# Attention stage of an mLSTM, MoE and MLP kernel: weight groups one per chunk from the second to the tenth, the inter bank read ahead of the state sums, q and k laid out contiguously

## The chip, the cores and the metric

The kernel runs on one core of one Trainium2 chip. The metric is device time in microseconds (us) of one execution; lower is better. One execution was also recorded by the hardware profiler, and all rows below come from that record. Engines are named as in the profile: PE (TensorE matmul; PEld is its weight load), DVE (VectorE), ACT (ScalarE), POOL (GpSimd), SP (SyncE, which here only issues DMAs).

## What is computed

Three layers in a row, all with f32 inputs. The change touches only the first, an mLSTM attention over B=2 batches, H=8 heads, S=768 steps, head size D=40:

```
for t in range(S):
    m_new = max(f[t] + m, i[t])
    C = exp(f[t] + m - m_new) * C + exp(i[t] - m_new) * outer(v[t], k[t])
    n = exp(f[t] + m - m_new) * n + exp(i[t] - m_new) * k[t]
    y[t] = sigmoid(o[t]) * (C @ q[t]) / max(abs(n . q[t]), 1)
```

Its output, 1536 tokens of 320 values, goes through a noisy top-2 mixture of 8 experts (`out += w * relu(x @ w1[e]) @ w2[e]`, hidden size 1024), and that result through a 2048-wide MLP with a relu6 gate.

## The kernel before

The order of the work on every engine is the order in which the program is written: nothing reorders it, and an engine that waits holds up all that stands behind it in its own queue. The recurrence is computed in chunks of 64 steps, 12 chunks, both batches side by side on the 128 partitions (64 rows each). Chunk n of the main loop (n = 0 to 9; the last two chunks are written out after it) does this:

- `pmul(n+1)` (L261): DVE multiplies the scores of chunk n+1 by their decay matrix, which frees the scores' PSUM bank for chunk n+2.
- `step(2)`: two pieces of the routing generator `route`, which handles two chunks' tokens at a time. It is started at the end of chunks 2, 4, 6, 8, so its first pieces stand in the odd chunks: a copy of the logits (L430), Abs and Exp on ACT (L433, L434), and DVE's `w<-u` (L439), which needs them.
- `inter(n)` (L281): 32 matmuls of q and k against the state `Sb`, written to bank 3, the inter bank. The same bank is used in each chunk, so PE may write it only after `norm_eg` of the chunk before has read it.
- `state(n)` (L291, L297): 32 matmuls of k and v into two banks, and two DVE sums that update `Sb`; then `decay` on POOL (L270).
- `load(n+3)` (L136): q, k, kv and the output gates of three chunks ahead, on SP's queue.
- `norm2(n-1)` (L361, L362, L364): tokens x of the chunk before, and their store to DRAM.
- `scores(n+2)` (L231), `values(n)` (L308), `expo(n+2)` (L238, L240, exponent on ACT L243), `xpose(n-1)` (PE transposes L388, ACT copies L390, L391) and `logits(n-1)` (L402).
- `scatter` (L414, L415): routing indices on POOL.
- weights of expert 0: `w_hi` casts one group on ACT (L593 or L598) into a high part, `w_lo` subtracts on DVE (L594 or L599) to get the low part, `w_load` loads the next group from DRAM (L589) into one of four `raw` buffers. A load into a buffer waits until the low part made from it is done. All three stand in chunks 3 to 7, `w_load` alone also before the loop and in chunks 0 to 2.
- `kscale(n+2)` (L255): eight ACT multiplies, in chunks 3 to 8.
- `norm_eg(n)` (L327): DVE reads the inter bank; `norm_pv(n)` (L334 to L346): DVE adds the values bank and prepares the denominator.
- `gate(n+1)`: a DVE max (L353), then Exp, Ln, Exp on ACT (L354 to L356).

On DVE, `norm_eg(n)` stands behind `w_lo`; `w_lo` needs ACT's cast, and this stands on ACT behind the copies of `xpose`, which need PE's transposes:

```
        scatter(3 if n == 8 else 2)
        if 3 <= n < 8:
            w_hi()
            w_lo()
        if n < 8:
            w_load()
        ...
        kscale(n + 2)
        norm_eg(n)
        step(2)
        norm_pv(n)
        gate(n + 1)
```

The mixture of experts starts after the loop and a tail that normalises, routes and gathers the last tokens; its first matmuls (L845) need expert 0's five weight groups.

Of the kernel before, what the change touches and what calls it, by code (L numbers as in the profile page):

```python
# [24 lines left out]
NT = 12  # L25
# [38 lines left out]
def mlstm_moe_mlp(ctx, tc, qk, kv, on, gf, gf6, wg, nz, w1, w2, w_in, w_out, cf, cb, cs, ci, out):  # L64
# [28 lines left out]
    identb, maskb, eyeb = cbt[:, 0:128], cbt[:, 128:192], cbt[:, 192:256]  # L93
    ltri, ones = cbt[:, 256:384], cbt[:, 384:512]

    QK = [att.tile([128, 4, 3, 128], F32, name=f"qk{i}") for i in range(4)]
    RWG = att.tile([128, 6, 2, 128], BF, name="RWG")
    Sb = att.tile([128, B, 4, V1], F32, name="Sb")
    SEL = const.tile([128, 8, B, 64], BF, name="SEL")
# [12 lines left out]

    def qk_parts(n):
        t = QK[n % 4]
        return [(t[64 * x:64 * x + 40, :, x:x + 2, :], qk[n, x]) for x in range(2)]

    def kv_part(n):
        kvt[n] = att.tile([128, H * (D + V1)], F32, name="kv", bufs=4)
# [94 lines left out]
    def step(k=1):  # L213
        for _ in range(k):
            for g_ in list(gens):
                if next(g_, "end") == "end":
                    gens.remove(g_)
# [6 lines left out]
    def scores(n, ps_=range(4)):  # L224
        q = QK[n % 4]
        if n not in s4t:
            s4t[n] = bank(3 if n == 1 else 0).rearrange("p (h t) -> p h t", h=8)
        s4 = s4t[n]
        for p in ps_:
            for b in range(B):  # L230
                T.matmul(s4[rows[b], 2 * p:2 * p + 2, :], q[:, p, 1, rows[b]], q[:, p, 0:3:2, rows[b]],  # L231
                         start=True, stop=True)

    def expo(n):
        e = bank(1)
        e3 = e.rearrange("p (h t) -> p h t", h=8)
        for b in range(B):
            T.matmul(e[rows[b]], rwg(0, n), SEL[:, :, b, :], start=True, stop=False, skip_group_check=True)  # L238
        for h in range(8):
            T.matmul(e3[:, h, :], SEL[:, h].rearrange("p b t -> p (b t)"), rwg(1, n), start=False, stop=True,  # L240
                     skip_group_check=True)
        d = att.tile([128, 8, 64], F32, name="dd", bufs=3)
        A.activation(d, e3, AF.Exp)  # L243
        Pt[n] = None, d
        if n + 1 < NT:
            k = att.tile([128, 8, D], F32, name="kt", bufs=3)
            kt[n] = k
            if n < 5:
                G.tensor_tensor(k, kvt[n][:, 0:DM].rearrange("p (h d) -> p h d", h=8),
                                d[:, :, 63:64].to_broadcast([128, 8, D]), OP.mult)  # L250
# [22 lines left out]
    def inter(n, bp=2, bi=3):  # L273
        q = QK[n % 4]
        vv = kvt[n][:, DM:].rearrange("p (h d) -> p h d", h=8)
        pv = bank(bp)[:, 0:8 * V1].rearrange("p (h d) -> p h d", h=8)
        it = bank(bi)[:, 0:8 * V1].rearrange("p (a c) -> p a c", a=4)
        for p in range(4 if n else 0):
            for x in range(2):
                for b in range(B):  # L280
                    T.matmul(it[rows[b], p, x * V1:(x + 1) * V1], q[:, p, 2 * x, rows[b]], Sb[:, b, p, :],  # L281
                             start=True, stop=True)
        y_ps[n] = (pv, it, vv)

    def state(n):
        Sd = Sds.pop(n, None)
        vv = y_ps[n][2]
        for b in range(B):
            for h in range(8):
                p, x = divmod(h, 2)  # L290
                T.matmul(stp[b][64 * x:64 * x + 40, p, :], kt[n][rows[b], h, :],  # L291
                         vv[rows[b], h, :], start=True, stop=True)
        spot[0] += 2
        step()
        for b in range(B):
            if n:
                V.tensor_tensor(Sb[:, b], Sd[:, b], stp[b], OP.add)  # L297
            else:
                V.tensor_copy(Sb[:, b], stp[b])
            step()  # L300
        if n + 2 < NT:
            decay(n + 1)
# [28 lines left out]
    def norm_pv(n):  # L331
# [15 lines left out]
        step()  # L347
        yt[n] = o, rd

    def gate(n):  # L350

        t = ont[n]
        V.tensor_scalar(t, t, -80.0, None, OP.max)  # L353
        A.activation(t, t, AF.Exp, scale=-1.0)  # L354
        A.activation(t, t, AF.Ln, bias=1.0)
        A.activation(t, t, AF.Exp, scale=-1.0)  # L356
# [49 lines left out]
    def cut_idx(e):  # L406
        assert len(scat) >= 2 * CUT[e], len(scat)
        nc.sync.dma_start(idx[(0, 3)[e]][:, 0:2, :], tab4[:, 0:2, :])
# [298 lines left out]
    def w_load():  # L707
        if pos[0] < len(queue):
            loaded.append(raw_load(queue[pos[0]][0]))
            pos[0] += 1  # L710
# [3 lines left out]
    def w_hi(k=1):  # L714
        for _ in range(k):
            los.append(queue[pos[1]][1](loaded[pos[1]]))
            pos[1] += 1

    def w_lo(k=1):
        for _ in range(k):  # L720
            los.pop(0)()
# [295 lines left out]
    load(2)  # L1017
    warm(WARM)
    scores(0)
    w_load()  # L1020
    warm(W[0])
    expo(0)
    pmul(0)
# [2 lines left out]
    decays()  # L1026
    warm(W[2])
    expo(1)
    gate(0)
    G.tensor_copy(adj, iota8)  # L1030
    warm(W[3])
    for n in range(NT - 2):
        pmul(n + 1)
        step(2)
        inter(n)
        state(n)
        if n + 3 < NT:
            load(n + 3)
        if n >= 1:
            norm2(n - 1)  # L1040
            step()
        scores(n + 2, range(2))
        values(n, range(4))
        expo(n + 2)
        values(n, range(4, 8))
        if n >= 1:
            xpose(n - 1)
        scores(n + 2, range(2, 4))
        scatter(3 if n == 8 else 2)
        if 3 <= n < 8:  # L1050
            w_hi()
            w_lo()
        if n < 8:
            w_load()
        if n + 3 >= NT:
            dummy(DUM[0], 1)
        if n >= 1:
            logits(n - 1)
        kscale(n + 2)
        norm_eg(n)  # L1060
        step(2)
        norm_pv(n)
        gate(n + 1)
        if n >= 2 and n % 2 == 0:
            gens.append(route(n // 2 - 1))
        if n == CUT[0] + 2:
            scatter(4)
            cut_idx(0)
    gate(NT - 1)
    n = NT - 2  # L1070
    pmul(n + 1)
# [162 lines left out]
def _arrays(inp):  # L1234
    import ml_dtypes
    q, k, v, o = [_np.asarray(inp[n]) for n in ('q', 'k', 'v', 'o_gate')]

    def bits(a):
        return _np.ascontiguousarray(a).view(_np.int64)

    def tr(a):
        return a.reshape(B, H // 2, 2, NT, 64, D).transpose(3, 2, 5, 1, 0, 4).reshape(NT, 2, D, H // 2, 128)

    def nat(a):
        return a.reshape(B, H, NT, 64, D).transpose(2, 0, 3, 1, 4).reshape(NT, 128, H, D)

    qt, kt = tr(q), tr(k)
    qk = _np.stack([_np.stack([qt[:, 0], kt[:, 0]], axis=3), _np.stack([kt[:, 1], qt[:, 1]], axis=3)], axis=1)
    vn = _np.concatenate([nat(v), _np.ones((NT, 128, H, 1), _np.float32)], axis=3)
    kv = _np.concatenate([nat(k).reshape(NT, 128, -1), vn.reshape(NT, 128, -1)], axis=2)  # L1250
    on = nat(o).reshape(NT, 128, H * D)
    gf = _np.stack([_np.asarray(inp[n]).reshape(16, S) for n in ('i_gate', 'f_gate')], axis=1)
    gf6 = gf.reshape(16, 2, 6, 128).transpose(0, 2, 1, 3).reshape(96, 2, 128)
    wgn = _np.zeros((384, 16), _np.float32)
    wgn[:320, :8] = inp['moe_w_gate']
    wgn[:320, 8:] = inp['moe_w_noise']
    wg = wgn.reshape(3, 128, 16).transpose(1, 0, 2)
    nz = _np.asarray(inp['moe_noise']).reshape(2, NT, 64, 8).transpose(0, 2, 1, 3).reshape(128, NT, 8)
    p = _np.arange(128)
    cf = _np.zeros((128, 147), _np.float32)  # L1260
    cf[:, 146] = -7.0 * 2 ** 30
    cf[:, :128] = _np.eye(128)
    cf[:, 128:136] = _np.arange(8)
    cf[64:, 144] = -1.0
    cf[:, 145] = 3.0
    mask = _np.where(_np.arange(64)[:, None] > _np.arange(64)[None], -1e30, 0.0)
    free = _np.concatenate([_np.arange(16, 32), _np.arange(48, 64), _np.arange(96, 128)])
    mk = _np.zeros((128, 128))
    mk[free] = _np.concatenate([mask, _np.eye(64)], axis=1)
    ltri = 8.0 * (p[:, None] < p[None])  # L1270
    cb = _np.concatenate([_np.eye(128), mk, ltri, _np.full((128, 128), 8.0)], axis=1).astype(ml_dtypes.bfloat16)
    sel = _np.zeros((128, 8, 2))
    for r in range(48):
        sel[r // 16 * 32 + r % 16, r % 8, r % 16 // 8] = 1.0
    cs = sel.reshape(128, 16).astype(ml_dtypes.bfloat16)
    ci = (_np.arange(NT)[None] * 128 + p[:, None]).astype(_np.int32)
    a = dict(qk=qk, kv=kv, on=on, gf=gf, gf6=gf6, wg=wg, nz=nz, w1=inp['moe_w1'], w2=inp['moe_w2'],
             w_in=bits(inp['moe2_w_in']).reshape(DM, 2, F).transpose(1, 0, 2).reshape(2 * DM, F), w_out=bits(inp['moe2_w_out']).reshape(2, 8, 128, DM).transpose(0, 2, 1, 3).reshape(256, 8 * DM), cf=cf, cb=cb, cs=cs, ci=ci)
    return {n: _np.ascontiguousarray(x) for n, x in a.items()}
# [16 lines left out]
```

## Time and profile before

| | us |
|---|---|
| median of 3 runs | 553.83 |
| lowest, highest of them | 552.12, 556.47 |
| the profiled execution, its own time | 558.33 |
| its span, first to last instruction | 556.5 |
| busy over the span: PE, PEld | 516.3, 460.8 |
| busy over the span: DVE, ACT, POOL | 340.5, 238.4, 127.2 |

The attention stage with its start takes about the first 120 us of the span, the tail to the first expert matmul another 16 us; the rest is the experts and the MLP. The share of busy time is a mean over stages with different limits. The granted clock is the share of TensorE's full 2.4 GHz that the chip gave: 1.00 or 0.50, and in a stretch with both something between.

### The profile page before, as it was taken

What the parts mean: (1) busy time and instruction counts of PE and PEld (TensorE: products, weight loads), DVE (VectorE), ACT (ScalarE), POOL (GpSimd) and SP (SyncE); (2) the same over time, 40 slices, a digit from 0 to 9 for tenths busy, and PEclk for the clock granted to TensorE, in tenths of its full rate; (3) what the DMA queues carried; (4) which work ended last, traced back from release to release, by engine and by line L of the source; (5) the groups of instructions that cost most, each with busy time, mean ns of one, the idle gap of its engine ahead of it and who ended that gap; (6) DMA issues with size and microseconds to landing.
All of it is one profiled execution on the core that took longest, in us unless ns stands there. A gap on an engine that the chain in (4) does not pass through costs nothing. (4 is left out here: it accounts for less than half of the span.)

```text
span 556.5 us, 11218 instructions
## 1 busy us (share of the span) xinstructions
PE 516.3 (93%) x4329; PEld 460.8 (83%) x4329; DVE 340.5 (61%) x853; ACT 238.4 (43%) x498; POOL 127.2 (23%) x165
## 2 busy tenths in 40 slices
PE   5878886996978999999999999999999999999996
PEld 2657665764978999999999989989988899999885
DVE  5354546655864487878787878547878534343433
ACT  0333555433444354545454545345654333333332
POOL 5231232525632220202020101078600100000000
PEclk9895755568988999999999999999999999999999
DMA  5793656501628667889897866976931600001011
GB/s 154 227 248 94 188 110 117 122 25 58 153 61 273 219 215 257 304 244 313 268 314 248 282 213 208 301 213 201 343 119 48 230 8 0 2 15 34 7 42 49
DMA packets 48073, 90.81 MB, mean 163 GB/s; under 512 B 7584, under 2 KB 32512, under 8 KB 48016
## 3 DMA queue, kind: packets, MB, share of 16 engines
q1 hardware_dynamic: 39976, 68.14, 40.3%
q0 software_dynamic: 6464, 19.94, 11.9%
q10 hardware_dynamic: 1576, 1.97, 1.2%
q8 instruction: 35, 0.57, 0.5%
q14 instruction: 22, 0.18, 0.1%
HBM read 66.77 MB, written 23.07 MB: 161 GB/s over the span
## 5 line engine op out<-in xcount | busy, mean ns | idle before, releaser
L860 DVE SCALAR_TENSOR_TENSOR r<-r,bank 128x512 f32<-128x512 f32 (+1 forms) x56 | 34.2, 611 | 81.7 <-ACT r L859 77.7
L845 PE MATMUL bank<-XH,SB 128*128 128x448 f32 (+3 forms) x280 | 78.9, 352 | 0.3 <-PEq L945 0.3
L848 ACT ACTIVATE hb<-bank 128x448 fp32r<-128x448 f32 (+2 forms) x80 | 37.4, 468 | 95.6 <-PE bank L845 77.9
L859 ACT ACTIVATE r<-bank,cft 128x512 f32<-128x512 f32 (+1 forms) x56 | 35.0, 626 | 96.9 <-PE bank L845 86.9
L845 PE MATMUL bank<-XL,SB 128*128 128x448 f32 (+3 forms) x192 | 68.8, 359 | 0.0
L881 PE MATMUL bank<-SB,hb 128*128 128x320 f32 x192 | 62.5, 326 | 3.0 <-ACT yo L916 1.4
L772 POOL DMA_INDIRECT XG<-Xd,idx x32 | 30.9, 966 | 133.6 <-PE bank L782 106.0
L881 PE MATMUL bank<-SA,hb 128*128 128x320 f32 x192 | 60.8, 316 | 0.0
L883 PE MATMUL bank<-SB,hb 128*128 128x320 f32 x192 | 60.1, 313 | 0.0
L882 PE MATMUL bank<-SB,hb 128*128 128x320 f32 x192 | 59.7, 311 | 0.0
L883 PE MATMUL bank<-SA,hb 128*128 128x320 f32 x192 | 59.4, 309 | 0.1
L882 PE MATMUL bank<-SA,hb 128*128 128x320 f32 x192 | 59.3, 309 | 0.0
L845 PE MATMUL bank<-XH,SA 128*128 128x448 f32 (+2 forms) x200 | 54.0, 342 | 2.0 <-ACT XH L783 2.0
L845 PEld LDWEIGHTS bank<-XH,SB 128*128 128x128 f32 x280 | 51.6, 193 | 5.1 <-issue 0.6
L845 PE MATMUL bank<-XL,SA 128*128 128x448 f32 (+2 forms) x120 | 40.9, 341 | 0.0
L845 PEld LDWEIGHTS bank<-XH,SA 128*128 128x128 f32 x200 | 37.2, 199 | 4.3 <-ACT XH L783 2.5
L881 PEld LDWEIGHTS bank<-SB,hb 128*128 128x128 f32 x192 | 36.6, 191 | 5.0 <-ACT hb L832 1.8
L594 DVE TENSOR_TENSOR SA<-raw,SA 128x1024 fp32r<-128x1024 f32 (+1 forms) x20 | 27.1, 1356 | 20.6 <-ACT SA L593 20.2
L845 PEld LDWEIGHTS bank<-XL,SB 128*128 128x128 f32 x192 | 37.0, 193 | 2.8
L882 PEld LDWEIGHTS bank<-SB,hb 128*128 128x128 f32 x192 | 36.6, 191 | 0.8
L881 PEld LDWEIGHTS bank<-SA,hb 128*128 128x128 f32 x192 | 36.1, 188 | 1.3
L882 PEld LDWEIGHTS bank<-SA,hb 128*128 128x128 f32 x192 | 36.1, 188 | 1.1
(201 smaller groups left out, 1141.3 us busy)
## 6 DMA issues: line engine op xcount, KB each, us to landing
raw<-in_w_dram SPq DMA_DIRECT2D x18, 640.0 KB
raw<-in_w_dram SPq DMA_DIRECT2D x18, 512.0 KB
craw<-in_w_in_dram SPq DMA_DIRECT2D x8, 640.0 KB
craw<-in_w_out_dram SPq DMA_DIRECT2D x8, 640.0 KB
raw<-in_w_dram SPq DMA_DIRECT2D x18, 256.0 KB
Yd<-yo SPq DMA_DIRECT2D x24, 160.0 KB
Yd<-zy SPq DMA_DIRECT2D x4, 880.0 KB
kv<-in_kv_dram SPq DMA_DIRECT2D x10, 324.0 KB
```

Source lines behind the costliest of these rows:

```text
L594: return lambda: eng.tensor_tensor(lo, t[:, 0:w], hi, OP.subtract)
L772: G.indirect_dma_start(out=XG[0:n, (u.xo + i) % 4, :], out_offset=None, in_=Xd[0:CUT[u.i] * 128] if early else Xd[:, :], in_offset=bass.In ...
L845: T.matmul(p, a, b, start=(i == 0), stop=(i == 7))
L848: A.activation(hb[:, 0:N], p, AF.Relu)
L859: A.activation(r, p, AF.Relu, bias=three)
L860: V.scalar_tensor_tensor(r, r, 6.0, p, OP.min, OP.mult)
L881: T.matmul(p, h, wh, start=s, stop=False)
L882: T.matmul(p, h, wl, start=False, stop=False)
L883: T.matmul(p, hb[:, lo:lo + 128], wh, start=False, stop=t)
```

## The change

- q and k: the SBUF tile changes from (pair, part, 128) to (part, pair, 128), and the arrays in DRAM with it, so that one partition's row of a load is one run of 1,024 values (4 KB) where it was four of 256 (1 KB). Bytes and matmuls stay.
- The weight loads move: none before the loop and none in chunk 0; one in each of the chunks 1 to 9 (before: one before the loop and one in each of the chunks 0 to 7). In a chunk they now stand ahead of `scores`.
- `w_hi` moves from chunks 3 to 7 to chunks 4 to 8, behind `kscale` and `gate`; `w_lo` of the same group follows in the next chunk (5 to 9), behind `norm2`.
- `norm_eg(n)` moves from the end of the chunk to right behind `inter(n)`, ahead of the state sums.
- DVE's max of the output gate becomes `gate_max(n+1)`, behind `norm_eg(n)`; the three ACT steps of `gate(n+1)` move ahead of `norm_pv(n)`.

```diff
-    QK = [att.tile([128, 4, 3, 128], F32, name=f"qk{i}") for i in range(4)]
+    QK = [att.tile([128, 3, 4, 128], F32, name=f"qk{i}") for i in range(4)]
...
-        return [(t[64 * x:64 * x + 40, :, x:x + 2, :], qk[n, x]) for x in range(2)]
+        return [(t[64 * x:64 * x + 40, x:x + 2], qk[n, x]) for x in range(2)]
...
+    def gate_max(n):
+        V.tensor_scalar(ont[n], ont[n], -80.0, None, OP.max)
...
     scores(0)
-    w_load()
     warm(W[0])
...
         inter(n)
+        norm_eg(n)
+        gate_max(n + 1)
         state(n)
         if n + 3 < NT:
             load(n + 3)
         if n >= 1:
             norm2(n - 1)
             step()
+        if 5 <= n:
+            w_lo()
+            w_load()
+        elif n:
+            w_load()
         scores(n + 2, range(2))
...
         scatter(3 if n == 8 else 2)
-        if 3 <= n < 8:
-            w_hi()
-            w_lo()
-        if n < 8:
-            w_load()
         if n + 3 >= NT:
             dummy(DUM[0], 1)
         if n >= 1:
             logits(n - 1)
         kscale(n + 2)
-        norm_eg(n)
+        gate(n + 1)
+        if 4 <= n < 9:
+            w_hi()
         step(2)
         norm_pv(n)
-        gate(n + 1)
```

The order on PE and on POOL stays the same, instruction by instruction. (In the changed kernel lines from 350 on carry numbers higher by 2.)

DVE in chunk 7, an odd one, from the first piece of the routing on; y<-bank,eG is `norm_eg`, Sb the state sums, x the tokens of chunk 6, SA the low part of a weight group. Before:

```order
L430 COPY zg<-bank_167 128x32
L439 TENSOR_SCALAR w<-u 128x16
L441 SCALAR_TENSOR_TENSOR w<-w,u 128x16
L297 TENSOR_TENSOR Sb<-Sd,bank_90 128x164
...
L361 TENSOR_TENSOR x<-od,rd 128x320
L447 TENSOR_TENSOR l<-l,nzt 128x16
L594 TENSOR_TENSOR SA_170<-raw,SA_170 128x1280
L327 TENSOR_TENSOR y<-bank_1297,eG 128x328
```

DVE in the same place now:

```order
L432 COPY zg<-bank_167 128x32
L441 TENSOR_SCALAR w<-u 128x16
L327 TENSOR_TENSOR y<-bank_1291,eG 128x328
L351 TENSOR_SCALAR on<-on 128x320
L443 SCALAR_TENSOR_TENSOR w<-w,u 128x16
L297 TENSOR_TENSOR Sb<-Sd,bank_90 128x164
...
L363 TENSOR_TENSOR x<-od,rd 128x320
L449 TENSOR_TENSOR l<-l,nzt 128x16
L601 SCALAR_TENSOR_TENSOR SA_169<-sth,cft,raw 128x1024
```

The read of the inter bank has gone from behind the low part to ahead of the state sums; it, the gate's max and all behind them now stand behind `w<-u`.

ACT from the end of chunk 6 into chunk 7; SA and sth are the casts of a weight group, kt is `kscale`, the three on<-on are `gate`, u the routing. Before:

```order
L390 COPY xT<-bank_1223 128x256
L391 COPY xT<-bank_1223 64x128
L593 CAST SA_170<-raw 128x1280
L255 ACTIVATE kt<-kv,dd 128x40 x8
L354 ACTIVATE on<-on 128x320
L355 ACTIVATE on<-on 128x320
L356 ACTIVATE on<-on 128x320
L433 ACTIVATE u<-zg 128x16
L434 ACTIVATE u<-u 128x16
```

ACT in the same place now:

```order
L392 COPY xT<-bank_1222 128x256
L393 COPY xT<-bank_1222 64x128
L255 ACTIVATE kt<-kv,dd 128x40 x8
L356 ACTIVATE on<-on 128x320
L357 ACTIVATE on<-on 128x320
L358 ACTIVATE on<-on 128x320
L600 CAST sth<-raw 128x1024
L435 ACTIVATE u<-zg 128x16
L436 ACTIVATE u<-u 128x16
```

The cast moved behind the scaling and the gate, and is of the group before; the same work as before stands ahead of `u`.

SP's queue from the loads of chunk 3 on, before:

```order
L589 DMA raw<-in_w_dram 128x1024
L136 DMA qk_86<-in_qk_dram 40x4x256 x2
L136 DMA kv<-in_kv_dram 128x648
L136 DMA on<-in_on_dram 128x320
L589 DMA raw<-in_w_dram 128x1024
L136 DMA qk_83<-in_qk_dram 40x4x256 x2
L136 DMA kv<-in_kv_dram 128x648
L136 DMA on<-in_on_dram 128x320
L364 DMA Xd<-x 128x384
L589 DMA raw<-in_w_dram 64x1024 x2
```

SP's queue from the loads of chunk 3 on, now:

```order
L136 DMA qk_86<-in_qk_dram 40x1024 x2
L136 DMA kv<-in_kv_dram 128x648
L136 DMA on<-in_on_dram 128x320
L136 DMA qk_83<-in_qk_dram 40x1024 x2
L136 DMA kv<-in_kv_dram 128x648
L136 DMA on<-in_on_dram 128x320
L366 DMA Xd<-x 128x384
L591 DMA raw<-in_w_dram 128x1024
```

The first two weight groups no longer stand ahead of the loads of chunks 3 and 4; the first comes where the third was.

## Rows read from the trace of the kernel before

**Rows 1.** The page: TensorE's granted clock, in tenths, in 40 slices.

```profile
PEclk9895755568988999999999999999999999999999
```

**Rows 2.** Windows: length; PE, PEld, DVE, ACT, POOL busy; clock, DMA share, GB/s.

```profile
24.66:31.04 6.38, 5.77 (x156) 4.63 (x152) 4.87 (x13) 2.77 (x7) 3.49 (x5) 1.00 0.99 296
...
41.39:52.64 11.25, 9.60 (x157) 7.56 (x149) 4.24 (x13) 5.10 (x17) 0.94 (x1) 0.50 0.22 66
...
73.39:85.36 11.97, 9.80 (x153) 7.79 (x154) 6.77 (x26) 5.90 (x17) 3.90 (x6) 0.50 0.65 132
85.36:97.39 12.03, 9.59 (x149) 7.59 (x150) 6.80 (x25) 6.23 (x19) 3.89 (x6) 0.50 0.79 131
97.39:107.70 10.31, 10.28 (x164) 8.33 (x166) 7.38 (x35) 4.17 (x14) 4.71 (x9) 0.50 0.79 162
107.70:120.89 13.19, 11.29 (x148) 7.84 (x144) 6.69 (x29) 4.96 (x17) 5.96 (x9) 0.50 0.08 20
120.89:136.30 15.41, 10.87 (x268) 7.97 (x261) 7.68 (x32) 5.30 (x19) 8.13 (x13) 0.94 0.20 60
```

**Rows 3.** Waits of PE, 36 to 121 us: total us, times, longest.

```profile
PE bank L281 <- DVE l L449: 5.9, 3, 2.4
PE bank L281 <- DVE oh L508: 4.5, 2, 2.3
PE bank L388 <- issue: 3.7, 1, 3.7
```

**Rows 4.** Timeline, end of chunk 6 and chunk 7: start, us, instruction, idle before.

```profile
80.68 0.90 PE L388 MATMUL bank<-cft,x 128*128 128x128 f32 x3
...
81.62 0.37 ACT L390 COPY xT<-bank 128x256 f32<-128x256 f32 x1 [1.24 <-PE bank L388]
...
82.05 1.26 ACT L593 CAST SA<-raw 128x1280 fp32r<-128x1280 f32 x1
...
82.56 0.65 PE L402 MATMUL bank<-wgt,xT 128*32 128x16 f32 x24
83.21 1.86 ACT L255 ACTIVATE kt<-kv,dd 128x40 f32<-128x40 f32 x8
83.34 1.49 DVE L594 TENSOR_TENSOR SA<-raw,SA 128x1280 fp32r<-128x1280 f32 x1 [5.16 <-ACT SA L593]
84.75 0.49 DVE L327 TENSOR_TENSOR y<-bank,eG 128x328 f32<-128x328 f32 x1
...
85.39 1.94 PE L281 MATMUL bank<-Sb,qk 128*64 128x41 f32 x32 [2.17 <-DVE oh L508]
...
87.55 0.47 ACT L354 ACTIVATE on<-on 128x320 f32<-128x320 f32 x1 [2.48 <-DVE on L353]
...
89.40 0.17 DVE L439 TENSOR_SCALAR w<-u 128x16 f32<-128x16 f32 x1 [1.25 <-ACT u L434]
...
90.34 0.48 DVE L361 TENSOR_TENSOR x<-od,rd 128x320 f32<-128x320 f32 x1
```

**Rows 5.** Windows by granted clock; columns as in rows 2.

```profile
39.20:56.00 16.80, 15.07 (x253) 12.11 (x254) 7.94 (x31) 7.65 (x24) 1.75 (x2) 0.50 0.41 121
56.00:62.90 6.90, 4.59 (x109) 3.58 (x108) 3.90 (x14) 4.60 (x15) 0.93 (x1) 0.99 0.51 140
...
120.70:134.70 14.00, 11.06 (x272) 8.12 (x268) 7.66 (x31) 5.09 (x18) 7.78 (x12) 0.99 0.22 66
18.80:35.50 16.70, 16.09 (x409) 12.46 (x409) 9.14 (x24) 7.91 (x19) 6.48 (x10) 1.00 1.01 271
```

**Rows 6.** DMA queues of SP (q1) and ACT (q10): packets, MB, share.

```profile
q1 hardware_dynamic: 39976, 68.14, 40.3%
...
q10 hardware_dynamic: 1576, 1.97, 1.2%
```

**Rows 7.** Timeline of SP's queue: two q and k loads, one kv load.

```profile
19.14 1.60 SPq L136 DMA_DIRECT2D qk<-in_qk_dram  x2
20.79 0.49 SPq L136 DMA_DIRECT2D kv<-in_kv_dram  x1
```

More of the change, by code (lines that the diff above doesn't have):

```diff
@@ L230, in scores @@
             for b in range(B):
-                T.matmul(s4[rows[b], 2 * p:2 * p + 2, :], q[:, p, 1, rows[b]], q[:, p, 0:3:2, rows[b]],
+                T.matmul(s4[rows[b], 2 * p:2 * p + 2, :], q[:, 1, p, rows[b]], q[:, 0:3:2, p, rows[b]],
                          start=True, stop=True)
@@ L280, in inter @@
                 for b in range(B):
-                    T.matmul(it[rows[b], p, x * V1:(x + 1) * V1], q[:, p, 2 * x, rows[b]], Sb[:, b, p, :],
+                    T.matmul(it[rows[b], p, x * V1:(x + 1) * V1], q[:, 2 * x, p, rows[b]], Sb[:, b, p, :],
                              start=True, stop=True)
@@ L348, in norm_pv @@
         yt[n] = o, rd
+    def gate_max(n):
+        V.tensor_scalar(ont[n], ont[n], -80.0, None, OP.max)
     def gate(n):
         t = ont[n]
-        V.tensor_scalar(t, t, -80.0, None, OP.max)
         A.activation(t, t, AF.Exp, scale=-1.0)
@@ L1028, in mlstm_moe_mlp @@
     expo(1)
+    gate_max(0)
     gate(0)
@@ L1068, in mlstm_moe_mlp @@
             cut_idx(0)
+    gate_max(NT - 1)
     gate(NT - 1)
@@ L1247, in _arrays @@
     qt, kt = tr(q), tr(k)
-    qk = _np.stack([_np.stack([qt[:, 0], kt[:, 0]], axis=3), _np.stack([kt[:, 1], qt[:, 1]], axis=3)], axis=1)
+    qk = _np.stack([_np.stack([qt[:, 0], kt[:, 0]], axis=2), _np.stack([kt[:, 1], qt[:, 1]], axis=2)], axis=1)
     vn = _np.concatenate([nat(v), _np.ones((NT, 128, H, 1), _np.float32)], axis=3)
```

## The prediction

> **What bounds the kernel now.** I read the page's slices first, for where PE runs slowly. The granted clock is at 8 or 9 tenths or above in every slice from the tenth on, and mostly at 5 to 7 in the fourth to ninth, which are the attention loop [rows 1]; there the change is made, so only that stretch needs a closer look. Next the windows from one `inter` to the next, for who is busy: chunk 6 (73.39 to 85.36) lasts 11.97 us, of which PE is busy 9.80 at half clock, DVE 6.77, ACT 5.90, POOL 3.90 [rows 2]. PE is the busiest engine and still idles about 2.2 us in it. Chunk 8, which has no weight group, lasts 10.31 us with PE busy for 10.28 [rows 2]: PE alone sets a chunk once nothing stops it.
>
> Then the waits of PE, for what stops it. Five times `inter` waits for DVE, 5.9 + 4.5 = 10.4 us in all [rows 3]. The names there, L449 and L508, are merely the instructions that DVE starts when L327 ends; the timeline shows the real chain. At the end of chunk 6 the transposes end at about 81.6, ACT copies them, casts the weight group (82.05, 1.26 us), DVE subtracts (83.34, 1.49 us, after 5.16 us of idling for that cast), and only then `norm_eg` reads the inter bank (84.75, 0.49 us). PE has finished the logits at 83.2 and starts `inter(7)` at 85.39 [rows 4]. So the weight group, work that attention doesn't need, stands on the path five times, once in each of chunks 3 to 7.
>
> Two other things take time there. PE stands still for 3.7 us for "issue", in the middle of the transposes of chunk 2 [rows 3], in a stretch where the DMA engines are at a share of 1.01 [rows 5]. And the clock, 1.00 from 18.8 to 35.5, is 0.50 from 39.2 to 56.0 [rows 5]: it fell after that standstill.
>
> **The change, part by part.** *`norm_eg` behind `inter`, low parts a chunk behind.* The inter bank is now read while PE does `state` and the scores, so the next `inter` finds it free. The five waits go: -10.4 us [rows 3]. The price on DVE is no new work, since each moved instruction was there before; the state sums come 0.49 us later for `norm_eg` and some 0.3 us for the gate's max, and the next `inter`, which needs them, is most of a chunk away. That cover is gone only if DVE falls a whole chunk behind, and its 6.8 us stand against PE's 9.6 to 9.8 [rows 2].
>
> *What is late next.* In odd chunks `w<-u` now stands ahead of `norm_eg`, the state sums and the tokens x, and it waits for ACT's u, behind which x and then PE's next transposes queue up. Before, it waited 1.25 us for u too [rows 4], with nothing urgent behind it. I set the new chain on the rows of chunk 7. ACT starts its copies at 81.62 and takes 0.43 until the next instruction, then the scaling 1.86, the gate 3 x 0.5, the cast 1.26 (now without a wait for the gate's max, which cost 2.48 before), the two routing steps about 0.5: u at 87.2. From `w<-u` to the end of x took 1.42 us (89.40 to 90.82); with `norm_eg` and the max in between it is 2.2, so x is ready at 89.4. PE, without its wait, would start the next chunk at 83.2 and reach its transposes 7.3 us later (in chunk 6 they start at 80.68 and the chunk at 73.39 [rows 2, 4]): 90.5. There are 1.1 us to spare, so the cost at half clock is 0. At full clock PE's share of this shrinks in the ratio of the chunks, 6.38 to 9.80 [rows 2]: it arrives at about 87.4 (81.6 + 0.65 x 8.9) and waits 2 us, in the three odd chunks behind a cast (5, 7, 9). The bounds are 0 and +6; I take +1, close to the half-clock end, since that clock rules this stretch in rows 2.
>
> *Weight loads.* Up to the standstill at 35.5 four groups were asked for, and now two. By the shapes in the order that is 1.15 MB less, at 271 GB/s [rows 5] about 4 us of transfer, as long as the standstill. If PE stood still because its own instructions were late behind data, which the trace doesn't show, the standstill goes (-3.7); if it has another cause it stays (0), or falls on another place, twice (+3.7). I take half of the gain, -1.9. With the standstill the fall of the clock would go: chunk 3 would then run at 6.4 instead of 9.7 us, -3.3, and again I take half, -1.6.
>
> *q and k contiguous.* SP needs 1.60 us to issue the two loads and 0.49 us for kv [rows 7], so perhaps 1 us less per chunk in a queue that PE doesn't wait for: 0. In transfer time, q10, where the q and k loads of two chunks are a large part, needs 1.2% x 16 x 556.5 / 1.97 = 54 us of engine time per MB and q1 40.3% x 16 x 556.5 / 68.14 = 53 [rows 6], so little can be won by longer runs: 0, with -1 and +1 at the start as bounds, as loads issued faster can also crowd the small transfers of the gates. The Trainium skill ("DMA: Bandwidth & Descriptors", Specifications) asks for at least 512 B per transfer for line rate, and 1 KB runs are above that; by this rule the layout gives nothing, and only the moved weight groups could relieve the stretch at 35.5. The two quotients agree.
>
> *Sum.* -10.4 + 1 - 1.9 - 1.6 = -12.9 us. The profiled execution took 558.3 us (span 556.5 and 1.8 around it), so 545.4 on its own scale. It lies 4.5 us above the median of 553.8, and I take the gain from the median: 540.9, so 541. What could make the difference smaller is that the standstill may belong to the profiled execution more than to the others.
>
> **The rivals.** *The clock stays high.* If the standstill and the five waits are gone, nothing stops PE for long and the clock of 1.00 could last. Chunks 3 to 9 take 41.39 to 120.89 = 79.5 us now. At full clock DVE's 6.8 us sets four of them and 6.4 + 2 = 8.4 the three odd ones behind a cast: 52.4, so -27.1 and 527 us. For it: from 18.8 to 35.5 PE was busy 16.09 of 16.70 us and kept 1.00 [rows 5]. Against it: from 39.2 on PE worked for over 11 us without a wait, and the clock stayed at 0.50 until 56.0 [rows 5]; chunk 8 had hardly an idle moment at 0.50 [rows 2]; and the fast spell from 56.0 to 62.9, with PE busy 4.59 of 6.90 us, ended behind a wait for `inter` of 2.3 us [rows 3, 5], about what odd chunks would get. The Trainium skill ("TensorE: Matmul & The Clock Gate", Loop structure matters more than you think) says that matmuls which follow each other without waits stay warm. By that rule this would be the likeliest result; the rows at 0.50 with a busy PE speak against it for matmuls as small as these.
>
> *The wait only moves.* DVE, not PE, could turn out to be the ring that closes: `w<-u` late, x late, the next product late, scores late. If 1.7 us of each of the five waits come back at the transposes or the scores, the gain is 10.4 - 8.5 = 1.9 and the time 552. For it: only 1.1 us to spare in odd chunks. Against it: DVE would have 3 us of idle time in a chunk of 9.8 [rows 2], and the gate's wait of 2.48 us on ACT goes.
>
> *Slower: the clock is lost early.* If after the first warm-up the clock isn't granted again at 18.8, or falls within the first chunks and returns only with the experts, the fast stretches of before cost the ratio 9.8 / 6.38 = 1.54: 16.09 us of PE work to 35.5 gives +8.7, the spell from 56 to 60 gives +2.2, the tail's 11.06 us up to +6.0 [rows 5], together +16.9. Against -10.4 + 1 this makes +7.5: 561. It decides from the point where those stretches lose more than 15 us. For it: the clock rose twice within this stage at moments that no change of the work marks. Against it: the warm-up matmuls are the same.
>
> **How the numbers follow.** Forecast 0.55 (541), clock high 0.22 (527), the wait moves 0.15 (552), slower 0.06 (561), and 0.02 for the rest. The forecast's own range is 535 to 547: the waits fixed, the standstill and the clock behind it all gone or all there. To hold 8 in 10 the range takes in most of the fast rival and part of the one where the wait moves: 526 to 552. About 1%, 5.5 us, is what a measurement of this kernel can tell from no change. Faster by more than that: all of the fast rival and nearly all of the forecast, 0.77; within it the moved wait and the forecast's slow edge, 0.16; slower 0.07.
>
> **What would show it right or wrong.** Right: in the changed profile PE's waits at L281 for DVE are gone, and the chunks with a weight group last as long as PE's work in them, 9.6 to 10 us at half clock. The standstill near 35 us is shorter or gone, and the clock falls later. Wrong: PE waits at the transposes (L390 in the new numbering) for x, or at the scores for the product of L261, by 1.5 us or more in each odd chunk; or the chunks are as short as predicted and the tail from chunk 10 to the first expert matmul, 15.41 us before [rows 2], has grown by what they gave.

## The result and the profile after

The changed kernel took 537.89 us (median of 4 runs, 533.89 to 547.75) against 555.15 us (552.12 to 560.05) for the kernel before in the same comparison: a ratio of 0.966, 95% interval 0.955 to 0.976. A second comparison, later in the study, gave 543.11 us and 0.981 (0.971 to 0.990). The forecast was 541. Some executions of a kernel take one per cent or more longer at a lower granted clock; the medians here are of all runs, the ratios leave those out.

The page of the changed kernel, its span and the granted clock in tenths over 40 slices:

```profile
span 536.7 us, 11208 instructions
...
PEclk9699655588989999999999999999999999999999
```

The profiled execution took 538.54 us, its span is 19.8 us shorter than before. The slices of the attention loop still show 5 and 6, as before [rows 1], so the change did not free the loop of the low clock. The windows from one `inter` to the next, chunks 1 to 9 and the tail, with the columns of [rows 2]:

```profile
26.78:32.82 6.04, 5.65 (x153) 4.52 (x150) 4.76 (x13) 2.68 (x7) 3.38 (x5) 1.00 0.52 146
...
39.03:45.90 6.87, 5.79 (x158) 4.63 (x150) 4.97 (x22) 3.23 (x12) 1.66 (x2) 1.00 0.80 230
45.90:52.02 6.12, 6.03 (x161) 4.81 (x154) 5.38 (x23) 4.52 (x18) 1.78 (x3) 1.00 0.80 202
52.02:60.55 8.53, 6.68 (x158) 5.17 (x150) 5.53 (x23) 6.43 (x24) 2.77 (x4) 0.82 0.64 193
60.55:70.28 9.73, 9.73 (x160) 7.75 (x154) 7.74 (x32) 5.47 (x19) 6.96 (x10) 0.50 1.01 190
70.28:79.80 9.52, 9.52 (x156) 7.55 (x151) 6.16 (x28) 5.91 (x21) 4.16 (x6) 0.50 0.68 155
...
89.55:100.03 10.48, 10.48 (x158) 7.68 (x151) 7.17 (x29) 6.92 (x20) 5.25 (x9) 0.50 0.14 31
100.03:116.78 16.75, 15.45 (x268) 12.18 (x260) 8.06 (x33) 4.58 (x18) 7.94 (x13) 0.64 0.32 98
```

Chunks 6 and 7 had PE busy for 9.80 of 11.97 and 9.59 of 12.03 us [rows 2]; now they last 9.73 and 9.52 us, and PE is busy in all of it. Where the 19.8 us came from, by the places of `inter` in the two timelines: chunks 3 to 9 took 79.5 us and take 61.0 (39.03 to 100.03), -18.5; chunks 1 and 2 took 16.7 and take 12.25, -4.5; the start to the first of these windows is 2.1 us longer, the tail 1.3 us longer (its clock was 0.94 and is 0.64), and the experts and the MLP behind it changed by 0.3 us. One border of [rows 2] needs putting right: `inter` of chunk 9 started at 107.17, not at 107.70, so chunk 8 takes 9.75 us in both kernels, and chunk 9 gives 3.2 us. There PE stood five times for "issue" before, 0.31 to 0.49 us each, between 110 and 113.3 us; the changed kernel's profile has none of these.

PE's waits in the loop and the tail (engine, line, releaser: total us, times, longest):

```profile
PE bank L390 <- DVE x L363: 1.9, 1, 1.9
PE bank L784 <- DMA XG<-Xd,idx: 1.1, 1, 1.1
PE bank L240 <- issue: 1.1, 1, 1.1
...
PE bank L390 <- issue: 0.4, 1, 0.4
```

The five waits at L281 for DVE [rows 3] are gone. New is one wait of 1.9 us at the transposes for x. This is the chain that the prediction put together, in chunk 5 of the changed kernel's timeline (start, us, instruction, idle before):

```profile
51.11 0.37 ACT L392 COPY xT<-bank 128x256 f32<-128x256 f32 x1 [0.41 <-PE bank L390]
...
51.54 1.86 ACT L255 ACTIVATE kt<-kv,dd 128x40 f32<-128x40 f32 x8
...
54.66 1.03 ACT L595 CAST SA<-raw 128x1024 fp32r<-128x1024 f32 x1
...
55.60 0.21 ACT L435 ACTIVATE u<-zg 128x16 f32<-128x16 f32 x1
...
56.09 0.17 DVE L441 TENSOR_SCALAR w<-u 128x16 f32<-128x16 f32 x1 [2.97 <-ACT u L436]
56.17 0.49 DVE L327 TENSOR_TENSOR y<-bank,eG 128x328 f32<-128x328 f32 x1
...
57.54 0.48 DVE L363 TENSOR_TENSOR x<-od,rd 128x320 f32<-128x320 f32 x1
...
58.08 0.90 PE L390 MATMUL bank<-cft,x 128*128 128x128 f32 x3 [1.85 <-DVE x L363]
```

Read it from the end: the transposes wait 1.85 us for x, x stands on DVE behind `norm_eg` and `w<-u`, and `w<-u` waited 2.97 us for ACT, where the scaling of k, the gate and the cast of a weight group stand ahead of u. The clock was 1.00 up to this wait and 0.50 behind it.

### The profile page after: what moved, and what is told of

Its sections match the earlier page's. It is cut to its first block, busy times and chain, and to the rows that moved or that the text cites. A ratio compares the mean times of both kernels' runs of the same rounds, so it can differ in the third digit from the quotient of the medians.

```text
span 536.7 us, 11208 instructions
## 1 busy us (share of the span) xinstructions
PE 510.0 (95%) x4329; PEld 456.3 (85%) x4329; DVE 339.2 (63%) x853; ACT 237.0 (44%) x498; POOL 129.8 (24%) x165
## 5 line engine op out<-in xcount | busy, mean ns | idle before, releaser
L847 PE MATMUL bank<-XH,SA 128*128 128x448 f32 (+2 forms) x200 | 52.4, 335 | 0.0
L847 PEld LDWEIGHTS bank<-XH,SA 128*128 128x128 f32 x200 | 35.9, 192 | 2.1 <-ACT XH L785 0.4
L856 DVE SCALAR_TENSOR_TENSOR hb<-bank,hb 128x64 fp32r<-128x64 f32 x64 | 14.1, 220 | 35.9 <-ACT hb L850 35.8
```

Source lines behind the costliest of these rows:

```text
L847: T.matmul(p, a, b, start=(i == 0), stop=(i == 7))
L856: V.scalar_tensor_tensor(hb[:, N:N + 64], p[:, o:N], 0.0, hb[:, o:N], OP.max, OP.subtract)
```

## The experiments

Ratios are to the kernel before in the same comparison, with 95% intervals.

**The read of the inter bank alone.** The kernel before with one edit:

```diff
         inter(n)
+        norm_eg(n)
         state(n)
...
         kscale(n + 2)
-        norm_eg(n)
```

> The kernel before with one edit: the read of the inter bank stands right behind inter. Theory A (the read's place is what held PE): the five waits at inter are gone and nothing takes their place, about 10 us faster than before. Theory B (the low part waiting for its own cast is what held PE, through DVE's order): the read is free, but the next product P still stands on DVE behind that low part. In chunk 7 of before P ended at 88.05; without the read ahead of it that is 87.6, while PE, started at 83.2, is ready for the scores at 86.2: a wait of 1.4 us at the scores in each of chunks 4 to 8, 7 of the 10.4 us come back, 3 to 4 us faster than before.

Measured: 553.0 us, ratio 1.003 (0.999 to 1.007): no gain. PE's waits in the loop and the tail in its profile:

```profile
PE bank L231 <- DVE P L261: 5.6, 6, 1.6
PE bank L476 <- DVE mk L465: 3.5, 3, 2.2
PE bank L240 <- issue: 1.6, 1, 1.6
PE bank L231 <- DVE l L445: 0.9, 1, 0.9
PE bank L388 <- issue: 0.9, 1, 0.9
```

The waits at `inter` are gone, and 5.6 + 3.5 + 0.9 = 10.0 us of waiting for DVE stand in their place (0.9 of it, for P, was there before): at the scores for the product P, and at the routing's matmuls for mk. One of them in its timeline, DVE held up by the low part as before, with 2 us of other DVE work between the low part and P:

```profile
79.77 1.49 DVE L594 TENSOR_TENSOR SA<-raw,SA 128x1280 fp32r<-128x1280 f32 x1 [4.75 <-ACT SA L593]
...
83.39 0.69 DVE L261 TENSOR_TENSOR P<-bank,dd 128x512 f32<-128x512 f32 x1
...
84.13 1.12 PE L231 MATMUL bank<-qk 128*64 128x128 f32 x8 [1.61 <-DVE P L261]
```

Theory B's mechanism holds, more fully than it expected: not 7 but about 9 of the 10.4 us come back, as mk was not on its list, and the 3 to 4 us that it left as a gain are not there.

**The weight groups alone.** The kernel before, with `w_load`, `w_hi` and `w_lo` in the places of the change and all else as before.

```diff
+        if 5 <= n:
+            w_lo()
+            w_load()
+        elif n:
+            w_load()
         scores(n + 2, range(2))
...
-        if 3 <= n < 8:
-            w_hi()
-            w_lo()
-        if n < 8:
-            w_load()
...
         kscale(n + 2)
+        if 4 <= n < 9:
+            w_hi()
         norm_eg(n)
```

> The kernel before with the weight groups alone moved as in the change (one load per chunk from 1 to 9, cast at the end of chunks 4 to 8, low part in the middle of the next chunk); the read of the inter bank stays at the end of the chunk, the layout of q and k stays. Theory A: the read at the end of the chunk still comes late, at least half of the waits at inter stay, under 6 us faster than before. Theory B: DVE no longer waits for a cast in front of the read, the waits at inter go without moving the read, 10 us or more faster than before, within 1% of the changed kernel.

Measured: 537.53 us, ratio 0.975 (0.968 to 0.982). PE's waits in the same stretch, the longest four:

```profile
PE bank L388 <- DVE x L361: 2.0, 2, 1.3
PE bank L231 <- DVE P L261: 1.9, 3, 0.7
PE bank L883 <- DVE hb L856: 1.3, 1, 1.3
PE bank L281 <- DVE l L449: 0.7, 1, 0.7
```

Of the 10.4 us at `inter` 0.7 are left, without the read moved; new are 2.0 us for x and 1.0 more than before for P. So the low part that waited for its own cast was the cause of those waits, and moving the weight groups is the whole of the gain that can be told from noise: the median is that of the changed kernel. This run moves the loads together with the casts and low parts; the run with early loads, below, has the loads where they were, no wait at `inter` either, and is still faster than before.

**The old layout of q and k**, in the changed kernel:

```diff
-    QK = [att.tile([128, 3, 4, 128], F32, name=f"qk{i}") for i in range(4)]
+    QK = [att.tile([128, 4, 3, 128], F32, name=f"qk{i}") for i in range(4)]
```

> The changed kernel with the old layout of q and k (runs of 1 KB). Theory that the layout gives nothing: within 1% of the changed kernel, the pause of PE in the transposes of chunk 2 stays under 1 us. Rival, that longer runs relieved the DMA engines: the pause is back at 2 us or more, the clock falls in chunk 2 or 3, and it takes 5 us or more longer than the changed kernel.

Measured: 538.65 us, ratio 0.980 (0.974 to 0.985); no pause for "issue" in chunks 2 and 3 at all, and the wait for x in chunk 5 is 1.9 us as with the new layout. The layout gives nothing that shows, and it did not relieve the pause.

**Early loads**, in the changed kernel: one weight load ahead of the loop, then one in each of chunks 0 to 2 and 5 to 9.

```diff
     scores(0)
+    w_load()
...
-        elif n:
+        elif n < 3:
             w_load()
```

> The changed kernel with the first four weight groups loaded as early as before: one ahead of the loop and one in each of chunks 0 to 2, none in chunks 3 and 4. Theory that PE's pause in chunk 2 comes from transfers asked for in the first chunks: the pause is back at 2 us or more, the clock falls there, chunks 3 and 4 run at about 9.7 us, and it takes 6 to 9 us longer than the changed kernel. Rival, that the pause has another cause: it stays under 1 us and the time within 1% of the changed kernel.

Measured: 545.09 us, ratio 0.984 (0.976 to 0.993). In its profile there is no pause in the transposes of chunk 2; one of 1.56 us stands in the expo of chunk 3, the clock fell behind it and chunk 3 took 8.7 us. The changed kernel has a pause of 1.08 us at the same instruction. The time lies between its two comparisons and the kernel before, and the interval overlaps the second of them: whether early loads cost something stays open. What it shows is that the 3.74 us of [rows 3] don't come back with them, and that with loads as early as before a gain of 1.6% is left.

**Which instruction pauses.** The kernel before once more, and the changed kernel with 16 more warm-up matmuls ahead of the first expo (the count `W[0]` from 4 to 20), which shift all that follows on PE by 16 matmuls and as many weight loads.

> The kernel before, unchanged, for a second profile. Theory that the pause of 3.74 us in the transposes of chunk 2 belongs to the order of before (four weight groups asked for early): it is there again, 3 us or more, at the same instruction, and the clock falls behind it. Rival, that the place is fixed and the size is chance: the pause is at the same instruction or at the fifth expo matmul of chunk 3, but of another size (0 to 2 us), and the clock falls elsewhere or not there.

> The changed kernel with 16 more warm-up matmuls ahead of the first expo and nothing else. They also shift PE's program by 32 instructions. Theory that PE's pauses for issue are where the next piece of its own program has to arrive: none at the third transpose of chunk 2 and the fifth expo matmul of chunk 3; if there are any, they come 16 matmuls earlier. The clock stays at 1.00 through the start: 0 to 3 us faster than the changed kernel up to chunk 5, and PE's wait for x in chunk 5 (about 1.9 us) is still there, with the fall of the clock behind it. Rival, that the pauses belong to the transposes and the expo themselves: they stay at these instructions.

PE's timeline at the pauses, first the kernel before in the profile of [rows 3]:

```profile
35.17 0.33 PE L388 MATMUL bank<-cft,x 128*128 128x128 f32 x1
39.25 0.58 PE L388 MATMUL bank<-cft,x 128*128 128x128 f32 x2 [3.74 <-issue]
```

The changed kernel:

```profile
36.96 0.44 PE L390 MATMUL bank<-cft,x 128*128 128x128 f32 x2
37.81 0.27 PE L390 MATMUL bank<-cft,x 128*64 128x128 f32 x1 [0.42 <-issue]
...
42.24 0.29 PE L240 MATMUL bank<-RWG,SEL 128*128 128x64 bf16 x4
43.60 0.28 PE L240 MATMUL bank<-RWG,SEL 128*128 128x64 bf16 x4 [1.08 <-issue]
```

The kernel before, second profile (555.12 us):

```profile
40.66 0.26 PE L240 MATMUL bank<-RWG,SEL 128*128 128x64 bf16 x3
42.61 0.32 PE L240 MATMUL bank<-RWG,SEL 128*128 128x64 bf16 x5 [1.69 <-issue]
```

The changed kernel with 16 more warm-up matmuls:

```profile
34.29 0.31 PE L308 MATMUL bank<-kv,P 64*64 64x41 f32 x2
34.88 0.60 PE L308 MATMUL bank<-kv,P 64*64 64x41 f32 x14 [0.29 <-issue]
...
39.19 0.42 PE L308 MATMUL bank<-kv,P 64*64 64x41 f32 x6
40.66 0.48 PE L308 MATMUL bank<-kv,P 64*64 64x41 f32 x10 [1.05 <-issue]
```

In the second profile of before the 3.74 us are not there; 1.69 us stand in the expo of chunk 3 instead. With the shift both pauses come 16 matmuls earlier: 14 of L308 and 2 of L390 lie between the first and its old place, 10 of L308, 2 of L238 and 4 of L240 between the second and its own. So the pauses belong to fixed places of PE's program and not to the instructions, to the layout or to a tile. From one to the other are 127 matmuls, 254 instructions with their weight loads. The page counts 35 transfers on its queue for instructions, and 2 x 4329 / 35 = 247, which suggests that PE pauses where the next piece of its program must arrive. The trace's record of that queue's transfers bears this out: the pause of 3.74 us in before ended at 39.25, and a transfer of 16,384 bytes had begun at 36.74, when PE already stood, and landed at 37.80. The other five pauses in the lines above ended in the same way, 1.3 to 1.5 us after such a transfer had landed. Where PE did not pause, at the first of the two places in the second profile of before, it had landed at 34.52, 1.6 us before PE went on there. So the pause is as long as that transfer is late; why it is late in one execution and not in the next stays open. Over the two places together the four profiles with early weight loads pause 1.6 to 3.7 us, the ten with later loads 0 to 2.7, which overlaps. The time of the shifted kernel was 542.97 us, ratio 0.977 (0.968 to 0.987), beside 543.11 and 0.981 (0.971 to 0.990) for the changed kernel: the same. Its profile has no wait for x in chunk 5, which its forecast had; the clock had fallen in chunk 3, as in two more variants below.

> The changed kernel, unchanged, beside the run with the warm-up on the same chip, and for a second profile: 1.5 to 2 us of waiting for x in chunk 5 if the clock is still high there, none if it fell earlier behind a pause for issue; within 1% of its first time.

Its profile (543.11 us) again shows the wait for x: 2.5 us in two waits, the longest 1.9, with the clock at 1.00 up to 56 us and 0.50 from 57 on.

**The wait for x.** Two edits of the changed kernel, alone and together: the cast behind the routing's u, and idle matmuls on PE where it waited.

```diff
         pmul(n + 1)
         step(2)
+        if 5 <= n:
+            w_hi()
         inter(n)
...
         gate(n + 1)
-        if 4 <= n < 9:
-            w_hi()
```

```diff
+        if n in (5, 7, 9):
+            dummy(8, 5)
         if n >= 1:
             xpose(n - 1)
```

> The changed kernel with the cast of a weight group one place later on ACT: behind the routing's steps u, in chunks 5 to 9, ahead of inter, instead of at the end of chunks 4 to 8. Theory (u behind the cast makes x late in the odd chunks): in the changed kernel the cast took 1.03 us ahead of u and PE waited 1.85 us for x in chunk 5; the wait shrinks to about 0.8 us. If the wait is what lost the clock there, the fast spell lasts past 60 us and the time falls by 3 us or more against the changed kernel; if not, the spell ends near 58 as before and the time is within 1%.

> The changed kernel with eight idle matmuls of 128x512 (results overwritten) on PE ahead of the transposes in chunks 5, 7 and 9, where PE waited 1.85 us for x in chunk 5; at full clock eight take about 1.7 us, at half 3.4. Theory that PE's wait in chunk 5 is what loses the clock: it stays at 1.00 past chunk 5, chunks 5 to 9 take 7 to 8.5 us instead of 9.7, 6 to 12 us faster than the changed kernel. Rival, that the small matmuls alone can't hold the clock: it falls within a chunk all the same, the idle matmuls then cost up to 3.4 us in each of two or three chunks at half clock, 3 to 8 us slower than the changed kernel.

> Both edits of the two runs before it: the cast behind u and eight idle matmuls ahead of the transposes in chunks 5, 7, 9. If the wait loses the clock, this holds it through the loop with less waiting than the idle matmuls alone: 8 to 15 us faster than the changed kernel. If small matmuls can't hold it, it is 0 to 6 us slower.

The cast alone: 540.98 us, ratio 0.974 (0.968 to 0.979). Its profile shows no wait for x, but doesn't test the theory: a pause of 1.90 us for "issue" in chunk 3 had taken the clock down by 44 us. The fill alone: 537.43 us, 0.972 (0.967 to 0.976); here too the profiled execution lost the clock in chunk 3, behind a pause of 1.35 us. Both within what the changed kernel showed, so neither theory can be read from them. Both together: 532.70 us, 0.968 (0.962 to 0.974). That is 5 or 10 us below the changed kernel's two medians, where 8 to 15 were expected, but the intervals overlap. In its profile the clock stays at 1.00 through chunk 5, which it had not in the changed kernel, and falls at about 76 us behind a pause of 1.75 us for "issue" in chunk 8.

With the idle matmuls came something that no theory above had: a lost clock returned behind them. In the profile of the fill alone, the 32 matmuls of `inter` ahead of the idle ones of chunk 5 and the 32 behind them:

```profile
55.41 1.93 PE L281 MATMUL bank<-Sb,qk 128*64 128x41 f32 x32
...
62.46 3.60 PE L317 MATMUL bank<-cbt 128*128 128x512 bf16 x8
...
67.97 1.13 PE L281 MATMUL bank<-Sb,qk 128*64 128x41 f32 x32
```

The clock was 0.50 from 43 us on and rose to 1.00 at 67.0, 0.9 us behind the end of the eight. In the four profiles with fill, those of the next runs included, five groups of idle matmuls ran at 0.50, and each time the clock rose between 0.4 us before and 1.0 us behind their end. In the eight profiles without fill of the changed kernel, its variants and the two parts run alone, a clock lost in the loop stayed at 0.50 for 41 to 79 us. That the idle matmuls are the cause is likely by this count, but no run was made to test it, and the kernel before got its clock back within the loop without them (at 56 us, and at 74 and 98 us in its second profile).

**Both edits and the longer warm-up.**

> The run before it, and 16 more warm-up matmuls of 128x512 ahead of the first expo, where PE stood idle for 4.14 us for the gates' transfer in the changed kernel and the clock fell to 0.50 until 23. Eighteen or so of these fit in the wait at full clock, so the end of the wait moves by 0 to 1 us. Theory that the idle wait costs the clock at the start: the clock stays at 1.00 from 9 us on and the first inter comes at about 23.5 to 25 instead of 26.8, 2 to 3 us faster than the run before it. Rival, the wait for the gates sets the start: no gain.

> The fastest variant so far, unchanged (cast behind u, eight idle matmuls ahead of the transposes of chunks 5, 7 and 9, 16 more warm-up matmuls), to see whether its time holds. It was 0.952 of before, the changed kernel 0.966 and 0.981 in two comparisons. If the lead is real: 0.945 to 0.962 of before, with no wait over 1 us for x in chunk 5 in the profile and the clock at 1.00 past chunk 5. If it was chance: 0.965 to 0.98.

Measured: 528.67 us (523.73 to 551.61 in five runs), ratio 0.952 (0.947 to 0.958), and on repetition 529.16 us (524.67 to 535.89 in six), 0.955 (0.951 to 0.960), in the range set for a real lead. This beats the kernel before, and very probably the changed kernel, beside which it was not run: its intervals overlap the low end of that kernel's first one (0.955 to 0.976) and lie below the second, and its medians are 9 to 14 us lower. The page of the repetition (528.56 us), granted clock:

```profile
PEclk9999979699699999999999999999999999999998
```

In the fourth to the eighth slice, about 40 to 107 us, the changed kernel had 9, 6, 5, 5 and 5; here it is 9, 9, 7, 9 and 6, and no wait for x is left. The first `inter` comes at 24.78 us, 24.59 with both edits alone: the warm-up keeps the clock at 1.00 from 8 us on, but the start is set by the transfer of the gates, as the rival said. Why it then gains 4 us, while the warm-up alone gained none, was not separated; the first profiled execution, 531.50 us, is hardly faster than the one without the warm-up, 531.71, and the profiles differ most in where PE paused.

## Why the prediction was right, and where not

**The sum.** 541 was forecast and 537.89 and 543.11 measured. The five waits, -10.4, went in full, and chunks 6 and 7 last as long as PE's work in them, as forecast. The nearness of the total is in part luck. In the profiled execution the other 9.4 of the 19.8 us are: chunks 3 to 5 -6.3, mostly by their higher clock, chunks 1 and 2 -4.5, chunk 9 -3.2, small differences -0.7, the new wait for x +1.9, start and tail +3.4. For the new wait the forecast had +1, for all the rest together -3.5.

**Whose merit it is.** The step named the move of `norm_eg` and that of the low parts in one term, and its argument was the read: "The inter bank is now read while PE does `state` and the scores". That attribution failed. The read alone gains nothing (1.003), the weight groups alone gain all (0.975 beside 0.966 and 0.981). What was on the path was DVE standing idle for a cast; PE waits for whichever of the instructions behind it is needed first, the read or the product P. The rival of the moved wait described just this, for the whole change; it is what happens to half of it.

**What is late next.** The wait for x was forecast at 0 for half clock and 2 us for full clock, in the odd chunks behind a cast. Measured are 1.85 us in chunk 5, at full clock, and none in chunks 7 and 9, at half. The term of +1 was 0.9 short, by this single wait.

**The weight loads.** The -1.9 and -1.6 rested on a pause of 3.74 us that, it was supposed, the early loads brought about. The first half of that thought, that PE's own instructions came late, agrees with the transfer that landed at 37.80. The second half was not borne out: the second profile of before has no such pause, and with early loads in the changed kernel it doesn't return. So the size of a pause in one execution was taken for a property of the kernel. The text saw this risk and took half. (The share of 1.01 that it set beside the pause is of the stretch up to 35.5, where the pause begins; in the pause the DMA engines were at 0.95.) That the clock stayed high through chunks 3 and 4 in both profiles of the changed kernel is what made up for it: 6.87 us instead of 11.25 for chunk 3, of which 1.69 is one of the five waits. In four profiles of its variants (early loads, cast alone, fill alone, warm-up alone) the clock fell in chunk 3, so that is not sure either.

**The layout** was priced at 0, and its removal showed nothing clear of noise (0.980 beside 0.966 and 0.981).

**The rival of the high clock** came true for chunks 3, 4 and most of 5, and ended at the very wait that was named against it. With that wait taken care of, idle matmuls and a longer warm-up, which is another kernel than the one forecast, it comes true for most of the loop (529 us; the rival's price was 527). The rival of the lost clock came true in a small part: the clock came back at 23 us instead of 19, and the first window starts 2.1 us later (0.9 in the second profile). The rule cited for it (the Trainium skill, "TensorE: Matmul & The Clock Gate", Loop structure matters more than you think), that matmuls following each other without waits stay warm, agrees with chunks 3 and 4 at 1.00. Chunks 6 to 9, where PE was busy for the whole of each window at 0.50, show what the forecast's doubt was about: in the changed kernel a PE without waits kept the clock that it had, and in these chunks did not get back the one it had lost.

## What to carry to other kernels

When an in-order engine stands idle for something that nobody needs yet, move that work to a place where its input is long ready; moving the one instruction that was seen to be late only hands the wait to the next one in the queue. Before crediting a change with the parts it lists, run each part alone. And take a second profile before pricing a stall that occurs once: what was 3.74 us in one execution was absent in the next.

## What was not expected of the hardware

PE's pauses for "issue" in chunks 2 and 3 stand at fixed places of its program, 254 instructions apart, moved by exactly 16 matmuls when 16 were added ahead, and were between 0 and 3.74 us long at the same place in different executions and variants; they ended 1.3 to 1.5 us after a transfer of the instruction queue had landed. Other pauses for "issue", such as the five in chunk 9 of before, don't stand at such distances and are not explained. In the loop the clock fell behind pauses or waits as short as 1.05, 1.35, 1.56, 1.69 and 1.90 us (issue) and 1.85 us (x), and stayed at 1.00 after others of 1.08 (twice), 1.51 and 1.56 us, so the length alone did not tell. Once fallen, the clock stayed at 0.50 for 54 us in the changed kernel (58 to 112 us), with PE busy without a gap in chunks 6 to 9; eight idle matmuls of 128x512, 3.2 to 3.6 us long at that clock, were followed by its return in five cases of five.
